# A squareplus gate formed on VectorE from PSUM instead of by a linear matrix on TensorE

## The chip, the cores and the metric

One core of one Trainium2 chip runs the kernel. Five engines work beside each other, each through its own instruction queue in order: TensorE (PE) multiplies matrices into PSUM, VectorE (DVE) and ScalarE (ACT) read and write both memories (PSUM and SBUF), GpSimd (POOL) works on SBUF, SyncE (SP) issues the DMAs. The metric is the device time of one execution in microseconds, and less is better. The engines wait for each other by semaphores; a profile records when each instruction ran.

## What is computed

A gated linear attention, then a two-layer MLP whose activation is squareplus. All inputs and the output are float32; the kernel multiplies in float16.

```python
# q, k, v, f_logit: (4, 8, 768, 48)
f = 1.0 / (1.0 + np.exp(-f_logit))
for t in range(S):
    state = f[:, :, t, :, None] * state + np.einsum('bhd,bhe->bhde', k[:, :, t], v[:, :, t])
    y[:, :, t] = np.einsum('bhd,bhde->bhe', q[:, :, t], state)
x = y.transpose(0, 2, 1, 3).reshape(3072, 384)
h = x @ w_in                            # 384 x 2048
g = 0.5 * (h + np.sqrt(h * h + 4.0))
out = g @ w_out                         # 2048 x 384
```

So g = 0.5 h + sqrt(0.25 h^2 + 1). The first term is linear in x, and both kernels differ in where it is formed.

## The kernel before

The 3072 tokens are 24 row blocks of 128, six for each of the four batch entries; two row blocks make a pair, and the MLP works by pairs (256 tokens), 12 of them.

**Attention, for each pair.** `add_logs`: ACT forms the log decays (Exp, then Ln), DVE splits them into a high and a low float16 part (`lhi`, L326; `llo`, L329). `add_decays`: PE sums them over the block with a triangular matrix into an h bank (L352 to L359, the "W" work), ACT takes two exponentials of the sums (`ea`, `eap`, L365), POOL multiplies them into q and k (`qk`, L371), DVE casts v (L377) and copies small sums (`nls`, L381). `add_attention`, for each row block: q and k are transposed, by PE and a DVE copy (L464, L468) for blocks below `XBAR_FROM` = 10, by a DMA issued by SP (L453) from there on; PE forms the scores (L488), DVE masks them (`pm`, L494), PE forms y (L509, L511), DVE casts it (L516), and it is transposed in turn (PE L544 and DVE L547, or DMA L535) into `xT`. `add_state` carries the state on (L563, L566, L572).

**MLP, for each pair.** `add_mlp1`, called M1 here: PE makes 48 matmuls of 256 columns (L652) into PSUM tiles `hps` of two banks; ACT squares a tile (L660, 1024 columns) and takes the root of two squared tiles (L668, 2048 columns). That root is the `g` tile: the linear half of the gate is not in it. `add_mlp2`, called M2: for each row block 16 matmuls with w_out (L686), and ahead of them three with `w_lin` (L683), all into one PSUM sum `o`; DVE evicts it (L694), SP stores it (L698).

**The linear matrix.** w_lin = 0.5 w_in w_out (384x384) is made once on the chip: `add_transposed_w_in` transposes w_in by PE (L598) and copies it (L604); `add_linear_part` multiplies (L621) and scales (L627). M2 of the first row block waits for it.

**PSUM** has eight banks: h has two tiles of two banks, "a" (all of the attention) two, o two. **The order** of the work is made ahead of time by the class `Plan`: every operation has an engine, a planned duration, a due time, and rings of buffers that it takes and frees, and `Plan.run` gives each engine's queue the ready operation that can start first, the one with the earlier due time among near ones. ACT has two tables of functions, one for Exp and Ln and one for Sqrt; the attention's ACT work is bundled in stretches by `GROUPS` to change tables seldom (L742, L744). Loads go through rings of four buffers (three for f), issued by SP in a fixed order with the weights between the first pairs; an SP instruction that waits holds up those behind it.

Of the kernel before, what the change touches and what calls it, by code (L numbers as in the profile page):

```python
# [15 lines left out]
GROUPS = [[0], [1], [2], [3], [4, 5], [6, 7], [8, 9], [10, 11]]  # L16

XBAR_FROM = 10

PACE = 15.5  # L20
LEAD = {"W": 45.0, "B": 26.0, "M1": 0.0, "M2": -30.0}


class Op:
    __slots__ = ("eng", "dur", "deps", "emit", "due", "allocs", "uses", "end", "kind", "dma", "ins")

    def __init__(self, eng, dur, emit, deps=(), due=0.0, allocs=(), uses=(), kind=None, dma=None, ins=()):
        self.eng, self.dur, self.emit, self.due, self.kind, self.dma = eng, dur, emit, due, kind, dma
# [18 lines left out]
class Plan:  # L47
# [33 lines left out]
    def run(self):  # L81
# [6 lines left out]
        for k in self.queues:  # L88
            by_eng.setdefault(k[0], []).append(k)
        stretch = None  # L90
        loose = False
        while left:
            best = None
            for eng, ks in by_eng.items():
                now = free.get(eng, 0.0)
                cands = []
                for k in ks:
                    if heads[k] < len(self.queues[k]):
                        op = self.queues[k][heads[k]]
                        t = self.ready(op)  # L100
# [11 lines left out]
                if eng == "ACT" and stretch is None and not loose:  # L112
# [38 lines left out]
            t, op, k, eng = best  # L151
            dur = op.dur
# [24 lines left out]
def kernel(  # L177
# [51 lines left out]
    w_lin = konst.tile([128, NJ, DM], FP16, name="w_lin")  # L229
# [14 lines left out]
    P = Plan()  # L244
    T = {}
# [27 lines left out]
    def add_weight(which, i):  # L273
# [17 lines left out]
        def cast():  # L291
            st = T["w", which, i]
            if which == "in":
                nc.vector.tensor_copy(out=w_in16[:, :, i * 256:(i + 1) * 256], in_=st.rearrange("p (j n) -> p j n", j=NJ))  # L294
            else:
                nc.vector.tensor_copy(out=w_out16[:, 2 * i:2 * i + 2, :], in_=st.rearrange("p (j n) -> p j n", j=2))

        w_ready[which, i] = P.add("wcast", "DVE", 0.55, cast, deps=[l], due=-10.0, uses=[buf])

# [8 lines left out]
    def add_logs(p, g):  # L308
# [16 lines left out]
        def d1():  # L325
            nc.vector.tensor_copy(out=lhi[p % NL][:, :, :, 0:D], in_=T["ls", p])  # L326

        def d2():
            nc.vector.tensor_tensor(out=llo[p % NL][:, :, :, 0:D], in0=T["ls", p],  # L329
# [4 lines left out]
        o1 = P.add("logs", "DVE", 0.6, d1, deps=[a2], due=due, allocs=[hl_b], uses=[ls_b])  # L334
        lg[p] = P.add("logs", "DVE", 1.0, d2, deps=[o1], due=due, uses=[ls_b])

    def add_decays(p, g):

        due = vtime(p, "W")
        h_b = Buf(ring("h", 2))  # L340
# [6 lines left out]
        def m1():  # L347
            h = pp_h.tile([128, 2, 512], FP32, name="hps", tag="hps")
            T["ca", p] = h
            for r in range(PR):  # L350
                ca = h[:, r, 0:H * D]
                nc.tensor.matmul(out=ca, lhsT=wcent, rhs=lhi[p % NL][:, r, :, 0:D], start=True, stop=False)  # L352
                nc.tensor.matmul(out=ca, lhsT=wcent, rhs=llo[p % NL][:, r, :, 0:D], start=False, stop=True)
            for r in range(PR):
                nl = h[:, r, H * D:H * D + 2 * NP].rearrange("p (j s) -> p j s", s=2)
# [421 lines left out]
```

## Time and profile before

| | us |
|---|---|
| median of 3 runs | 242.16 (242.06 to 242.81) |
| the profiled execution | 242.64 |
| its span | 240.9 |
| PE busy | 209.4 |
| ACT busy | 149.2 |
| DVE busy | 134.4 |
| POOL busy | 47.6 |

The span runs from the first to the last instruction of the profiled execution. A busy time is the time in which at least one instruction of that engine ran. Matmuls overlap in the pipeline, so their single durations add up to more than the engine's busy time, and the pace is better read from the chain of work, where a row says how long a run of matmuls kept the chain. The idle time before a group of instructions is put down to whatever came last.

### The profile page before, as it was taken

Reading aid. Unit: us, or ns where it says so; the run is one execution under the profiler, and the core shown is the slowest. Engines: PE = TensorE matmul, PEld = TensorE weight load, DVE = VectorE, ACT = ScalarE, POOL = GpSimd, SP = SyncE. Lnnn points to the kernel's source line nnn. Section 1 sums busy time; section 2 is a strip of 40 time slices with the busy share of each in tenths; the row PEclk is TensorE's granted clock in tenths of the full one; section 3 lists DMA queues with packets and bytes.
Section 4 is the critical chain, followed back from the end, with each engine's and each line's share of the span. In section 5 each row is a group of like instructions: output and inputs, shape, how many; then the busy total and the mean of one; then the engine's idle time right before and its main releaser. Section 6 shows DMA issues by size and latency. Waiting matters only on the chain.

```text
span 240.9 us, 4922 instructions
## 1 busy us (share of the span) xinstructions
PE 209.4 (87%) x2038; PEld 151.1 (63%) x2038; DVE 134.4 (56%) x243; ACT 149.2 (62%) x143; POOL 47.6 (20%) x36
## 2 busy tenths in 40 slices
PE   0372698799999994999599999999999999999994
PEld 0151575667668563677487577786678777777662
DVE  5559987866659759665941788435551444100110
ACT  4331264920499939946999399985399665667500
POOL 4236000130014164054100560005230000000000
PEclk9997587799999999799999999999999999999998
DMA  7999998999999979999996433331843111110011
GB/s 147 220 230 304 303 377 187 205 203 183 195 199 217 212 183 221 189 198 214 202 172 124 95 77 84 88 64 49 137 94 62 34 52 49 49 35 33 33 68 65
DMA packets 129302, 35.25 MB, mean 146 GB/s; under 512 B 121088, under 2 KB 129280, under 8 KB 129280
## 3 DMA queue, kind: packets, MB, share of 16 engines
q1 hardware_dynamic: 129280, 34.94, 65.9%
q8 instruction: 16, 0.26, 0.4%
q14 instruction: 6, 0.05, 0.1%
HBM read 25.17 MB, written 4.72 MB: 124 GB/s over the span
## 4 chain that ended last, share of the span: by engine, by line
PE 74%; DVE 12%; ACT 3%; issue 3%; DMA 3%; POOL 2%; SPq 1%; POOLq 0%; ACTq 0%
PE o L686 25%; PE hps L652 24%; PE o L683 5%; PE sc L488 4%; PE wl L621 3%; DVE pm L494 2%; PE tr L464 2%; DVE lhi L326 2%; PE y L511 2%; POOL qk L371 2%; DMA ld_q<-in_q_dram 2%; DVE v L377 1%; PE hps L352 1%; DVE w_in L294 1%; PE wtp L598 1%
## 5 line engine op out<-in xcount | busy, mean ns | idle before, releaser
L652 PE MATMUL hps<-xT,w_in 128*128 128x256 f16 x576 | 75.5, 279 | 5.2 <-ACT hsq L660 4.2
L686 PE MATMUL o<-w_out,g 128*128 128x384 f16 x384 | 73.9, 326 | 0.0
L660 ACT ACTIVATE hsq<-hps 128x1024 f16<-128x1024 f32 x48 | 48.3, 1018 | 36.1 <-PE hps L652 35.6
L652 PEld LDWEIGHTS <-w_in 128*128 128x128 f16 x576 | 55.9, 100 | 17.2 <-issue 5.1
L686 PEld LDWEIGHTS <-g 128*128 128x128 f16 x384 | 35.8, 98 | 20.5
L371 POOL TENSOR_TENSOR qk<-ld_q,ea 128x768 f16<-128x768 f32 x12 | 21.9, 1827 | 128.4 <-ACT ea L365 106.0
L668 ACT ACTIVATE g<-hsq 128x2048 f16<-128x2048 f16 x24 | 45.8, 1910 | 0.6
L494 DVE TENSOR_TENSOR pm<-sc,mask 128x512 f16<-128x512 f32 x48 | 31.9, 686 | 18.4 <-PE sc L488 18.3
L694 DVE COPY o_sb<-o 128x384 f32<-128x384 f32 x24 | 13.3, 556 | 40.3 <-PE o L686 39.8
L365 ACT ACTIVATE ea<-hps 128x768 f32<-128x768 f32 x12 | 9.7, 811 | 27.2 <-PE hps L359 27.2
L371 POOL TENSOR_TENSOR qk<-ld_k,eap 128x768 f16<-128x768 f32 x12 | 23.2, 1936 | 0.0
L516 DVE CAST y<-y 128x384 f16<-128x384 f32 x24 | 13.3, 554 | 17.3 <-PE y L511 17.2
L488 PE MATMUL sc<-qkT 48*128 48x128 f16 x192 | 15.5, 227 | 2.7 <-DVE xT L547 1.4
L683 PE MATMUL o<-w_lin,xT 128*128 128x384 f16 x72 | 15.9, 330 | 0.0
L488 PEld LDWEIGHTS <-qkT 48*128 48x128 f16 x192 | 8.8, 97 | 10.8 <-issue 10.0
L318 ACT ACTIVATE ld_f<-ld_f 128x768 f32<-128x768 f32 x12 | 10.1, 838 | 8.8 <-DMA ld_f<-in_f_logit_dram 8.8
L352 PE MATMUL hps<-lhi,wcent 128*128 128x384 f16 x24 | 8.6, 358 | 6.9 <-DVE lhi L326 6.9
L572 DVE TENSOR_TENSOR sn<-u,gam 128x384 f16<-128x384 f32 x20 | 11.0, 552 | 6.2 <-PE u L566 6.2
L511 PE MATMUL y<-v,pm 128*128 128x48 f16 x192 | 11.7, 185 | 1.1 <-DVE pm L494 1.1
L464 PE MATMUL tr<-ident,qk 128*128 128x128 f16 x80 | 7.7, 257 | 5.6 <-POOL qk L371 4.1
L326 DVE CAST lhi<-ls 128x768 f16<-128x768 f32 x12 | 11.0, 913 | 2.9 <-ACT ls L323 2.9
L511 PEld LDWEIGHTS <-pm 128*128 128x128 f16 x192 | 10.0, 98 | 3.1 <-issue 2.0
(58 smaller groups left out, 221.6 us busy)
## 6 DMA issues: line engine op xcount, KB each, us to landing
ld_f<-in_f_logit_dram SPq DMA_DIRECT2D x24, 192.0 KB, 3.8
ld_q<-in_q_dram SPq DMA_DIRECT2D x24, 192.0 KB, 3.8
ld_k<-in_k_dram SPq DMA_DIRECT2D x24, 192.0 KB, 4.0
ld_v<-in_v_dram SPq DMA_DIRECT2D x24, 192.0 KB, 3.9
out_dram<-o_sb SPq DMA_DIRECT2D x24, 192.0 KB, 1.9
ld_q<-in_moe_w_in_dram SPq DMA_DIRECT2D x3, 384.0 KB, 5.9
ld_k<-in_moe_w_in_dram SPq DMA_DIRECT2D x3, 384.0 KB, 6.1
ld_q<-in_moe_w_out_dram SPq DMA_DIRECT2D x3, 384.0 KB, 8.1
```

Of the source, the lines that this page charges most:

```text
L326: nc.vector.tensor_copy(out=lhi[p % NL][:, :, :, 0:D], in_=T["ls", p])
L371: nc.gpsimd.tensor_tensor(out=qk[p % NB][:, :, i, :, 0:D], in0=T[name, p], in1=T[e, p], op=ALU.mult)
L488: nc.tensor.matmul(out=t[:, j, :], lhsT=qkT[o:o + D, NP + j, :], rhs=qkT[o:o + D, j, :], start=True, stop=True)
L494: nc.vector.tensor_tensor(out=T["pm", r][:, s], in0=T["sc", r, s], in1=mask16.unsqueeze(1).broadcast_to([128, NP, C]), op=ALU.mult)
L511: nc.tensor.matmul(out=y[:, j, s], lhsT=T["pm", r][:, s, j, :], rhs=T["v16", p][:, i, 2 * j + s, :], start=(c == 0), stop=(c == 0 or s == 1))
L516: nc.vector.tensor_copy(out=y16.rearrange("p a b -> p (a b)"), in_=T["y", r].rearrange("p a b d -> p (a b d)"))
L652: nc.tensor.matmul(out=hb[:, a, :], lhsT=w_in16[:, j, jn * 128:(jn + 1) * 128], rhs=T["xT", p][:, j, :], start=(j == 0), stop=(j == NJ - 1))
L660: nc.scalar.activation(out=T["hsq", p, j8][:, j4 % 2], in_=T["h", p, j4].rearrange("p a n -> p (a n)"), func=AF.Square, scale=1.0)
L668: nc.scalar.activation(out=T["g", p][:, 8 * j8:8 * j8 + 8, :].rearrange("p a t -> p (a t)"), in_=T["hsq", p, j8].rearrange("p a n -> p (a ...
L683: nc.tensor.matmul(out=T["o", p, i], lhsT=T["xT", p][:, j, i * C:(i + 1) * C], rhs=w_lin[:, j, :], start=(j == 0), stop=False)
L686: nc.tensor.matmul(out=T["o", p, i], lhsT=T["g", p][:, jn, i * C:(i + 1) * C], rhs=w_out16[:, jn, :], start=False, stop=(jn == NN - 1))
L694: nc.vector.tensor_copy(out=T["o_sb", p, i], in_=T["o", p, i])
```

## The change

The matrix w_lin goes, with the transposes of w_in, the product, its three matmuls in each row block of M2 and two evictions. M1's PSUM tiles become single banks in a ring of five (`NH`), freed later: ACT squares each bank (512 columns), takes the root of a pair of banks (1024 columns) into a tile `r16`, and DVE then forms the gate in one instruction from the bank and the root (L666 of the changed kernel). The o ring shrinks from two banks to one (`NO`). The decays' sums take two of the five h banks, and their exponentials are cut in two. XBAR_FROM goes from 10 to 14, so four more row blocks are transposed by PE. Some operations may run on one of two or three engines, `"DVE|ACT|POOL"` with a planned duration for each, and the planner gives them to the one that would finish first. Tiles are taken by the instruction that begins a step (PE's) instead of the one that writes them. Groups and lead times of the decays change. The core of the diff:

```diff
-GROUPS = [[0], [1], [2], [3], [4, 5], [6, 7], [8, 9], [10, 11]]
-XBAR_FROM = 10
+GROUPS = [[0], [1], [2], [3], [4], [5, 6], [7, 8], [9, 10], [11]]
+XBAR_FROM = 14
-LEAD = {"W": 45.0, "B": 26.0, "M1": 0.0, "M2": -30.0}
+LEAD = {"W": 30.0, "B": 26.0, "M1": 0.0, "M2": -30.0}
+GATE = 10.0
+NH, NA, NO = 5, 2, 1
...
+                own = [c for c in cands if c[2][0].split("|")[0] == eng]
+                kept = []
+                for c in cands:
+                    if c[2][0].split("|")[0] != eng:
+                        first = c[2][0].split("|")[0]
+                        c[1].eng = first
+                        t1 = max(free.get(first, 0.0), self.ready(c[1])) + c[1].durs[first]
+                        c[1].eng = eng
+                        if t1 <= c[0] + c[1].durs[eng] + 0.1 or any(o[0] <= c[0] + 0.2 for o in own):
+                            continue
+                    kept.append(c)
...
-    pp_h = ctx.enter_context(tc.tile_pool(name="pp_h", bufs=2, space=PSUM))
-    pp_a = ctx.enter_context(tc.tile_pool(name="pp_a", bufs=2, space=PSUM))
-    pp_o = ctx.enter_context(tc.tile_pool(name="pp_o", bufs=2, space=PSUM))
+    pp_h = ctx.enter_context(tc.tile_pool(name="pp_h", bufs=NH, space=PSUM))
+    pp_a = ctx.enter_context(tc.tile_pool(name="pp_a", bufs=NA, space=PSUM))
+    pp_o = ctx.enter_context(tc.tile_pool(name="pp_o", bufs=NO, space=PSUM))
...
-        w_ready[which, i] = P.add("wcast", "DVE", 0.55, cast, deps=[l], due=-10.0, uses=[buf])
+        w_ready[which, i] = P.add("wcast", "DVE|ACT|POOL", {"DVE": 0.5, "ACT": 0.75, "POOL": 0.9}, cast, deps=[l], due=-1.0, uses=[buf])
...
-        o1 = P.add("logs", "DVE", 0.6, d1, deps=[a2], due=due, allocs=[hl_b], uses=[ls_b])
-        lg[p] = P.add("logs", "DVE", 1.0, d2, deps=[o1], due=due, uses=[ls_b])
+        o1 = P.add("hi", "DVE|POOL", {"DVE": 0.6, "POOL": 0.9}, d1, deps=[a2], due=due, allocs=[hl_b], uses=[ls_b])
+        lg[p] = P.add("lo", "POOL|DVE", {"DVE": 1.0, "POOL": 1.9}, d2, deps=[o1], due=due, uses=[ls_b])
...
-                nc.scalar.activation(out=t.rearrange("p r h d -> p r (h d)"), in_=T["ca", p][:, :, 0:H * D],
-                                     func=AF.Exp, scale=sign)
+                for r in range(PR):
+                    nc.scalar.activation(out=t[:, r].rearrange("p h d -> p (h d)"), in_=T["ca", p, r][:, 0:H * D],
+                                         func=AF.Exp, scale=sign)
...
-        d1 = P.add("v16", "DVE", 0.6, vc, deps=[ld["v", p]], due=due, allocs=[v_b], uses=[ld_buf["v", p]])
+        v_op = P.add("v16", "POOL|DVE", {"DVE": 0.6, "POOL": 0.9}, vc, deps=[ld["v", p]], due=due, allocs=[v_b], uses=[ld_buf["v", p]])
...
-        yc_op = P.add("Y", "DVE", 0.55, yc, deps=[o], due=due + 4.0, allocs=[y16_b], uses=[a_b])
+        yc_op = yc_ops[r] = P.add("Yc", "DVE|ACT", {"DVE": 0.55, "ACT": 0.5}, yc, deps=[o], due=due + 4.0, uses=[a_b])
...
-    wiT = {}
-    def add_transposed_w_in():
...
-    def add_linear_part(t_ops):
...
+        for j4 in range(4):
+            hsq_b, r_b = Buf(ring("hsq", 2)), Buf(ring("r16", 2))
+            sq, h_bs = [], []
+            for a in range(2):
+                j2 = 2 * j4 + a
+                h_b = Buf(ring("h", NH))
+                h_bs.append(h_b)
...
+                    nc.scalar.activation(out=T["hsq", p, j4][:, a], in_=T["h", p, j2], func=AF.Square, scale=1.0)
...
+                nc.scalar.activation(out=T["r16", p, j4], in_=T["hsq", p, j4], func=AF.Sqrt, scale=0.25, bias=1.0)
...
+                    nc.vector.scalar_tensor_tensor(out=T["g", p][:, jn:jn + 2, :].rearrange("p a t -> p (a t)"),
+                                                   in0=T["h", p, 2 * j4 + a], scalar=0.5, in1=T["r16", p, j4][:, a],
+                                                   op0=ALU.mult, op1=ALU.add)
+                go = P.add("G", "DVE", 0.65, gate, deps=[ro], due=due + 3.6 * j4 - GATE,
+                           allocs=[g_b] if a == 0 and j4 == 0 else [], uses=[r_b, h_bs[a]])
...
-                        for j in range(NJ):
-                            nc.tensor.matmul(out=T["o", p, i], lhsT=T["xT", p][:, j, i * C:(i + 1) * C],
-                                             rhs=w_lin[:, j, :], start=(j == 0), stop=False)
...
-            oo = P.add("o", "DVE", 0.55, oc, deps=[last], due=due - 20.0, allocs=[os_b], uses=[o_b])
+            oo = oc_op[p, i] = P.add("ev", "DVE|ACT", {"DVE": 0.55, "ACT": 0.5}, oc, deps=[last], due=due - 20.0, allocs=[os_b], uses=[o_b])
```

In the planner's new lines, an operation's first-named engine is its own; another takes it only where it would end earlier there and has no work of its own ready.

Where the change moves instructions, first DVE's queue in the first 50 us. Before, at the end of the weight casts (`w_out`), with the copies of the transposed w_in (`wiT`) and the scaling of `w_lin` behind them:

```order
L494 TENSOR_TENSOR pm<-sc,mask_80 128x512
L296 CAST w_out_95<-ld_v 128x768
L494 TENSOR_TENSOR pm<-sc,mask_80 128x512
L296 CAST w_out_95<-ld_q 128x768
L604 COPY wiT<-wtp 128x768
L296 CAST w_out_95<-ld_k 128x768
L516 CAST y_612<-y 128x384
L604 COPY wiT<-wtp 128x768 x7
```

Now, at the same stage of the work (`g` is the gate, `r` the root):

```order
L612 TENSOR_TENSOR sn<-u,gam_108 128x384
L666 SCALAR_TENSOR_TENSOR g_476<-hps,r_451 128x512 x2
L553 CAST y_479<-y 128x384
L612 TENSOR_TENSOR sn<-u,gam_108 128x384
L666 SCALAR_TENSOR_TENSOR g_476<-hps,r_505 128x512 x2
L588 COPY xT<-yt 128x3x128
L553 CAST y_540<-y 128x384
L666 SCALAR_TENSOR_TENSOR g_476<-hps,r_554 128x512 x2
L588 COPY xT<-yt 128x3x128
L326 CAST w_out_95<-ld_k 128x768
```

The copies of wiT have gone, and pair 0's gates stand between the attention steps of the next row blocks, the first of them ahead of DVE's four casts of w_out.

Second, ACT's queue where a stretch of exponentials ends and the MLP goes on (`hsq` is the square). Before:

```order
L660 ACTIVATE hsq<-hps 128x1024
L744 ACT_TABLE_LOAD
L668 ACTIVATE g_1650<-hsq 128x2048
L660 ACTIVATE hsq<-hps 128x1024 x2
L668 ACTIVATE g_1650<-hsq 128x2048
```

Now:

```order
L649 ACTIVATE hsq<-hps 128x512 x2
L741 ACT_TABLE_LOAD
L658 ACTIVATE r_2365<-hsq 128x1024
L649 ACTIVATE hsq<-hps 128x512 x2
L658 ACTIVATE r_2426<-hsq 128x1024
```

Squares and roots are half as wide and twice as many, and a root writes `r16`, which DVE reads, instead of the tile that M2 reads. The queue has 16 table loads now, 14 before.

Third, SP's queue around the last loads. Before:

```order
L266 DMA ld_f<-in_f_logit_dram 128x8x48 x2
L453 DMA_TRANSPOSE qkT<-qk_98 128x8x128 x2
L266 DMA ld_q<-in_q_dram 128x8x48 x2
L698 DMA out_dram<-o_sb 128x384
L266 DMA ld_k<-in_k_dram 128x8x48 x2
L266 DMA ld_v<-in_v_dram 128x8x48 x2
```

Now:

```order
L698 DMA out_dram<-o_sb 128x384 x2
L296 DMA ld_q<-in_q_dram 128x8x48 x2
L296 DMA ld_k<-in_k_dram 128x8x48 x2
L296 DMA ld_v<-in_v_dram 128x8x48 x2
L484 DMA_TRANSPOSE qkT<-qk_99 128x8x128 x2
L698 DMA out_dram<-o_sb 128x384
```

The first DMA transposes stood between the loads; now they stand behind the last one.

On POOL 18 instructions come on: seven casts of v, five of weights and six lo subtractions. ACT takes six evictions of o, three casts of y and two of w_in. In PE's queue the next row block's M2 begins right behind the last one's, with no other PE work between, at seven of the 23 changes of block, the last three among them.

## Rows read from the trace of the kernel before

**Rows 1.** The page's busy us, share of the span and instructions, by engine.
```profile
PE 209.4 (87%) x2038; PEld 151.1 (63%) x2038; DVE 134.4 (56%) x243; ACT 149.2 (62%) x143; POOL 47.6 (20%) x36
```

**Rows 2.** Windows by stage: start:end, length, busy us (instructions), granted clock, DMA, GB/s.
```profile
0.00:45.00 45.00, 24.20 (x245) 17.91 (x246) 34.99 (x66) 18.85 (x21) 10.58 (x16) 0.85 0.98 249
45.00:225.00 180.00, 172.94 (x1719) 125.98 (x1719) 97.19 (x174) 127.48 (x122) 37.01 (x20) 0.98 0.63 128
225.00:240.90 15.90, 12.28 (x76) 7.17 (x74) 2.23 (x4) 2.90 (x2) 0.00 (x0) 0.96 0.18 63
```

**Rows 3.** Windows of 20 us, the same columns.
```profile
60.00:80.00 20.00, 20.00 (x206) 14.37 (x204) 14.35 (x24) 16.13 (x16) 3.59 (x2) 1.00 0.98 201
80.00:100.00 20.00, 15.69 (x151) 11.00 (x151) 14.31 (x24) 15.46 (x18) 7.97 (x4) 0.91 1.01 208
100.00:120.00 20.00, 17.84 (x205) 13.05 (x204) 13.60 (x25) 14.09 (x16) 7.18 (x4) 1.00 0.98 197
...
140.00:160.00 20.00, 19.89 (x202) 14.84 (x201) 12.89 (x26) 18.02 (x19) 3.37 (x2) 1.00 0.41 88
```

**Rows 4.** The chain that ended last: start us, us, what (x matmuls).
```profile
29.42 3.76 PE hps L652 x24
...
47.43 1.31 PE wtp L598 x12
...
50.88 6.50 PE wl L621 x40
...
61.89 0.65 PE o L686 x4
...
76.00 0.89 PE tr L464 x16
...
108.62 2.77 DMA ld_k<-in_k_dram
...
224.27 0.66 PE hps L652 x6
224.93 0.49 PE o L683 x3
...
237.31 0.56 DVE o_sb L694
```

**Rows 5.** Instruction groups by shape: out<-in, count, busy us, mean ns, idle before.
```profile
L660 ACT ACTIVATE hsq<-hps 128x1024 f16<-128x1024 f32 x48 | 48.3, 1018 | 36.1 <-PE hps L652 35.6
L668 ACT ACTIVATE g<-hsq 128x2048 f16<-128x2048 f16 x24 | 45.8, 1910 | 0.6
...
L494 DVE TENSOR_TENSOR pm<-sc,mask 128x512 f16<-128x512 f32 x48 | 31.9, 686 | 18.4 <-PE sc L488 18.3
...
L516 DVE CAST y<-y 128x384 f16<-128x384 f32 x24 | 13.3, 554 | 17.3 <-PE y L511 17.2
...
L326 DVE CAST lhi<-ls 128x768 f16<-128x768 f32 x12 | 11.0, 913 | 2.9 <-ACT ls L323 2.9
...
L365 ACT ACTIVATE ea<-hps 128x768 f32<-128x768 f32 x12 | 9.7, 811 | 27.2 <-PE hps L359 27.2
```

**Rows 6.** Timelines of ACT, DVE, POOL, SP: start us, us, instruction, idle before.
```profile
65.69 1.28 ACT L744 ACT_TABLE_LOAD   x1
66.99 1.91 ACT L668 ACTIVATE g<-hsq 128x2048 f16<-128x2048 f16 x1
...
73.36 1.75 DVE L326 CAST lhi<-ls 128x768 f16<-128x768 f32 x1 [0.42 <-ACT ls L323]
...
76.02 0.55 DVE L326 CAST lhi<-ls 128x768 f16<-128x768 f32 x1
...
72.87 1.82 POOL L371 TENSOR_TENSOR qk<-ld_k,eap 128x768 f16<-128x768 f32 x1
...
103.22 3.19 SPq L453 DMA_TRANSPOSE qkT<-qk  x2
```

**Rows 7.** Waits on PE by DVE: us in total, times, longest.
```profile
DVE pm L494 <- PE sc L488: 18.3, 21, 2.4
```

More of the change, by code (lines that the diff above doesn't have):

```diff
@@ L88, in run @@
         for k in self.queues:
-            by_eng.setdefault(k[0], []).append(k)
+            for e in k[0].split("|"):
+                by_eng.setdefault(e, []).append(k)
         stretch = None
@@ L244 @@
     P = Plan()
+    eng_of = {"DVE": nc.vector, "POOL": nc.gpsimd}
+    cp = {"DVE": nc.vector.tensor_copy, "POOL": nc.gpsimd.tensor_copy, "ACT": nc.scalar.copy}
     T = {}
@@ L456, in add_attention @@
         else:
-            a_b = Buf(ring("a", 2))
+            a_b = Buf(ring("a", NA))
             def tp():
+                new("qkT", [128, 2 * NP, C], FP16, 3)
                 tr = pp_a.tile([128, 2 * NP, C], FP16, name="tr", tag="a")
@@ L610 @@
-    lin_ops = []
-    def add_linear_part(t_ops):
-        for j in range(NJ):
-            o_b = Buf(ring("o", 2))
-            last = None
-            for n in range(4):
-                def mm(j=j, n=n):
-                    if n == 0:
-                        T["wl", j] = pp_o.tile([128, DM], FP32, name="wl", tag="o")
-                    for jn in range(4 * n, 4 * n + 4):
-                        nc.tensor.matmul(out=T["wl", j], lhsT=wiT[jn // 8][:, jn % 8, j * 128:(j + 1) * 128],
-                                         rhs=w_out16[:, jn, :], start=(jn == 0), stop=(jn == NN - 1))
-                last = P.add("M2", "PE", 0.66, mm, deps=t_ops[4 * (n // 2):4 * (n // 2) + 4] + [w_ready["out", 2 * n], w_ready["out", 2 * n + 1], last],
-                             due=5.0, allocs=[o_b] if n == 0 else [], uses=[bufs["wiT", n // 2]])
-            def sc(j=j):
-                nc.vector.tensor_scalar(out=w_lin[:, j, :], in0=T["wl", j], scalar1=0.5, scalar2=None, op0=ALU.mult)
-            lin_ops.append(P.add("o", "DVE", 0.55, sc, deps=[last], due=5.0, uses=[o_b]))
+        o = P.add("KV", "PE", 0.34, kv, deps=[dec[p][0], dec[p][1], state_op.get(r), gm[r]], due=due, allocs=[a_b, sn_b], uses=uses)
@@ L631 @@
+        state_op[r + 1] = P.add("KV", "DVE", 0.55, dk, deps=[o], due=due, uses=[a_b])
     g_ops = {}
+    oc_op = {}
+    yc_ops = {}
     def add_mlp1(p):
@@ new lines, in add_mlp1, with half, square, root @@
+        for j4 in range(4):
[5 more added lines that the diff above has]
+                h_bs.append(h_b)
+                def half(j2=j2):
+                    T["h", p, j2] = pp_h.tile([128, 512], FP32, name="hps", tag="hps")
+                    hb = T["h", p, j2].rearrange("p (a t) -> p a t", a=2)
+                    for a in range(2):
+                        jn = 2 * j2 + a
+                        for j in range(NJ):
+                            nc.tensor.matmul(out=hb[:, a, :], lhsT=w_in16[:, j, jn * 128:(jn + 1) * 128],
+                                             rhs=T["xT", p][:, j, :], start=(j == 0), stop=(j == NJ - 1))
+                def square(a=a, j2=j2, j4=j4):
+                    if a == 0:
+                        T["hsq", p, j4] = sp.tile([128, 2, 512], FP16, name="hsq", tag="hsq", bufs=2)
+                    nc.scalar.activation(out=T["hsq", p, j4][:, a], in_=T["h", p, j2], func=AF.Square, scale=1.0)
+                o = P.add("M1", "PE", 0.66, half, deps=xT_ops[p] + [w_ready["in", j2]], due=due + 1.8 * j2,
+                          allocs=[h_b], uses=[bufs["xT", p]])
+                sq.append(P.add("M", "ACT", 0.54, square, deps=[o], due=due + 1.8 * j2,
+                                allocs=[hsq_b] if a == 0 else [], uses=[h_b]))
+            def root(j4=j4):
+                T["r16", p, j4] = sp.tile([128, 2, 512], FP16, name="r16", tag="r16", bufs=2)
+                nc.scalar.activation(out=T["r16", p, j4], in_=T["hsq", p, j4], func=AF.Sqrt, scale=0.25, bias=1.0)
+            ro = P.add("R", "ACT", 1.06, root, deps=sq, due=due + 3.6 * j4 + 1.8, allocs=[r_b], uses=[hsq_b], kind=("M", 0))
+            for a in range(2):
+                def gate(a=a, j4=j4):
+                    if a == 0 and j4 == 0:
+                        T["g", p] = sp.tile([128, NN, TB], FP16, name="g16", tag="g", bufs=4)
+                    jn = 4 * j4 + 2 * a
+                    nc.vector.scalar_tensor_tensor(out=T["g", p][:, jn:jn + 2, :].rearrange("p a t -> p (a t)"),
[3 more added lines that the diff above has]
+                           allocs=[g_b] if a == 0 and j4 == 0 else [], uses=[r_b, h_bs[a]])
+            g_ops[p].append(go)
```

194 lines of the change are left out of this document (77 added, 117 removed).

## The prediction

> **What bounds the kernel now.** I began with the busy shares of the page [rows 1]: TensorE (PE) is busy for 209.4 us of 240.9, ScalarE (ACT) 149.2, VectorE (DVE) 134.4, GpSimd (POOL) 47.6. A share is an average, so the windows by stage came next [rows 2]. Until 45 us, while data arrive, PE is busy for only 24.2 us and DVE for 35.0 of 45. From 45 to 225 PE works for 172.9 of 180 us, ACT for 127.5 and DVE for 97.2: there PE is the bound, and what leaves PE's queue there shortens the span, if the others keep up. From 225 on only M2 (the second matmul) and its stores are left. The chain that ended last agrees, since from 45 us on it is mostly PE pieces [rows 4]. The one other soft place is 80 to 120 us, where PE idles for 4.3 and 2.2 us [rows 3] and the chain runs through a load of k [rows 4].
>
> The profiled execution took 242.64 us, its span 240.9; 1.74 us lie around it. The median of the three runs is 242.16, so I add 1.74 to a span and take off 0.48 for the time to be forecast.
>
> **What leaves PE.** Three things. The linear term in M2 (L683): 24 row blocks with three matmuls each, 0.49 us for three [rows 4], 11.8 us; 20 of the blocks (9.8 us) lie ahead of the last M1 (the first matmul), 4 (2.0 us) behind. The product w_in by w_out (L621): 48 matmuls at 6.50 / 40 us, 7.8 us. The transposes of w_in (L598): 48, at 1.31 us for 12, 5.2 us [rows 4]. PE works without a break there and the chain runs through all three, so I count them in full: 24.8 us. What is late next at 50 us is M2 of pair 0, whose gates and weights are there by then, and M1 of pair 1, which stand in the order in their place; so the hole gets filled.
>
> **What PE gains.** Row blocks 10 to 13 are now transposed on PE instead of by DMA. 16 transposes of q and k took 0.89 us [rows 4], so a block's 8 cost 0.45, its 3 of y about 0.25: 2.8 us for four. A single o bank: the first M2 quarter of a row block must wait until the last block's sum is evicted. One eviction takes 0.56 us [rows 4], with the handover some 0.65. In the new order 7 of the 23 changes of block have no other PE work between them, three of these in the tail: 4.6 us if nothing hides them, 2.6 of it ahead of the last M1. PE alone then gives 240.9 - 24.8 + 2.8 + 4.6 = **223.5 us**. Bounds for the bank: 0, were all of it covered (the tail's three can't be), to twice that if evictions stand behind other work in the DVE queue.
>
> **What moves ahead of the first M1.** M1 begins at 29.4 us [rows 4], behind a string of DVE work. Two y casts of 0.55 us [rows 5] go from there to ACT, which idles: -1.1 us. Weight casts leave as well, but the loads that feed them are no faster (the DMA engines are 98% busy until 45 us [rows 2]), so I count nothing for them; bounds 0 and -2.2 (twice the y casts).
>
> **The load stream.** At 103.2 us the SP queue issued two DMA transposes, which took 3.19 us, between loads [rows 6], and at 108.6 the chain stands on a load of k [rows 4]. Now all loads are issued ahead of the first DMA transpose. That can give back up to the 6.5 us that PE idled from 80 to 120 [rows 3], or nothing, if the loads then wait for buffers that a busier ACT frees later. I take half: -3.2.
>
> **What ACT and DVE gain.** The gate: 96 DVE instructions that read 128x512 float32 from PSUM and a float16 operand from SBUF. The mask product pm has the same shape and types, 686 ns [rows 5]: 65.9 us. Up to 8 evictions for the transposes on PE add at most 5.5 at the same price. Some 40 DVE instructions go (wiT, w_lin, and casts, lo subtractions and evictions handed to ACT and POOL), at 0.55 us or more each [rows 5], 22 us. DVE rises from 134 to about 183 us. On ACT each long instruction is cut in two. Between 768 columns (811 ns) and 1024 (1018) a column costs 0.81 ns [rows 5], so about 0.19 us of each is fixed: 48 more squares 9.1 us, 24 more roots 6.0 (1910 ns for 2048 leaves 0.25), 24 more exponentials 4.6. Eleven casts and evictions add some 6, and two more table loads 2.6 (1.28 each, and the next instruction starts 1.30 us after the load began [rows 6]). ACT rises from 149 to about 177 us.
>
> The Trainium skill (ScalarE: Activation LUTs, What ACT_TABLE_LOAD costs) puts a switch of tables at about 2.66 us, a drain included; this trace doesn't show the drain, and by the page the two loads would cost ACT 5.3 us instead of 2.6.
>
> How much of this reaches the end? By PE, the last M1 would end at 224.9 - 22.8 (9.8 + 7.8 + 5.2) + 2.8 + 2.6 - 1.1 - 3.2 = 203.2 us. ACT would have about 150 us of work from 43.9 us (45 - 1.1) on: 127.5 [rows 2] plus 23, since the rest of the 28 falls ahead. Its densest window of the four is 18.02 of 20 us, 90% [rows 3]; at that share it needs 167 us, until 210.9, 7.7 later than PE. Five h banks and M2 work in hand let PE run ahead of ACT, so I take half, **+3.8**; bounds 0 and 7.7. The tail stays as it was: 16.0 us from the last M1 to the end [rows 4], less 2.0 for the linear term, plus 2.0 for the o bank.
>
> Sum: 223.5 - 1.1 - 3.2 + 3.8 = **223.0 us** of span, 224.7 as a run, **224.3** against the median.
>
> **Rivals.** *B, the covers hold better.* The load stream stops stalling PE, the mid-run o waits lie under other work, and ACT is never late: 223.5 - 1.1 - 6.5 - 2.6 = 213.3 of span, 214.6. For it: PE did 172.9 of 180 us in the long stage [rows 2], so its order was followed closely. Against it: all three engines would stand near 85% of the span, which only PE does now [rows 1].
>
> *A, ACT (or DVE beside it) is the bound.* If ACT can only be kept busy at the mean of its windows 60 to 80 and 140 to 160, (16.13 + 18.02) / 40 = 85% [rows 3], it needs 150 / 0.85 = 176 us, the last M1 ends at 220 and the span is 236, 237.4. For it: the exponent stretches, in which ACT stands between M1 and the roots, number eight as against seven, and in each ACT waits for PE and DVE. Against it: much of ACT's idle time before was PE's slowness, and that shrinks.
>
> *D, POOL blocks DVE.* The cast lhi took 0.55 us at 76.0, but 1.75 at 73.4, where POOL had an instruction running from 72.9 to 74.7 [rows 6]. The change puts 18 more instructions on POOL. If each held a DVE instruction up by the full 1.2 us, DVE would have 21.6 us more: about 163 us from 43.9 on, at 90% 181, the last M1 at 225 and the span at 241, 242.3: no change. Against it: the mean of lhi is 913 ns [rows 5], so a third of the full delay was usual; and pm, like the gate, kept its 686.
> The Trainium skill says the same of the mechanism (SBUF — State Buffer, Who interferes with whom): VectorE's two-port copies and GpSimd exclude each other for a whole instruction, while a VectorE instruction with one SBUF input does not meet GpSimd at all. By that rule the casts handed to POOL save DVE little, and the gate is safe; the rows agree on both.
>
> *C, the ring of h banks turns into the bound, and the kernel is slower.* A bank is now freed by the gate, not by the square. Least hold: two fills of 0.66 [rows 4], square 0.6, root 1.06, gate 0.69, about 3.7 us; the decays' 24 holds need some 3.3 (79 bank-us). Five banks from 29.4 us to the old last M1 at 224.9 give 978 bank-us, so the ring decides against the change once the mean hold of M1's 96 banks passes (978 - 79) / 96 = 9.4 us. The exponent stretches add about 2.3 (8 of them, each two table loads and some eight instructions of 0.8 us, 9 us on three banks, over 96), so it takes 3.4 us more on every gate, from standing in the DVE queue behind attention steps that wait for PE. At 4 us the last M1 ends at 29.4 + (79 + 96 x 10) / 5 = 237 and the span is 253, 254. Against it: pm, the commonest of such waiters, waited 21 times, 18.3 us in all, 2.4 at the longest [rows 7].
>
> That the change doesn't do what it says can be left out: the orders show the gates, and no linear matrix.
>
> **How the numbers follow.** The forecast case (219 to 229) gets 0.52; B (below 219) 0.17; A (229 to 241.4) 0.17; D (about no change) 0.04; C (slower) 0.10. The likeliest is 224.3. The range 214 to 239 leaves out 0.04 of B, 0.02 of A, and D and C, 0.20 together. Within 0.3% (0.7 us) a measurement of this kernel can't be told from no change: faster 0.52 + 0.17 + 0.17 = 0.86, same 0.04, slower 0.10.
>
> **What would show it.** PE: no wtp and wl rows, M2 of pair 0 near 46 to 50 us instead of 61.9 [rows 4]; the last M1 at 203 to 207; PE busy for some 183 us. The gate at 0.65 to 0.70 us; squares near 0.60, roots near 1.07. In the tail three gaps on PE of about 0.65 us between row blocks. If A holds, PE's longest waits name squares or gates and ACT's share from 45 us on passes 85% with PE under 85%; if D, lhi, v and gi grow well past their means; if C, M1 waits for the gate with DVE waiting for PE. B shows as PE above 96% from 45 us to the last M1. I am wrong from the start if PE finds no work in the hole at 50 us: then PE's gap there stays and the gain is some 13 us smaller.

## The result, and the profile after

| | before | after |
|---|---|---|
| median, us | 242.11 (241.91 to 242.81) | 230.98 (228.29 to 231.78) |
| the profiled execution, us | 242.64 | 230.96 |
| its span, us | 240.9 | 229.2 |

The ratio of the times is 0.950, with an interval of 0.942 to 0.958. The change gains 11 us at the medians. I had forecast 224.3, a gain of 17.8, with a range of 214 to 239: the direction and the range hold, the size is 6.7 us off. The time lies where rival A was (229 to 241).

The page of the changed kernel begins with the busy us, share and instructions of each engine, and then shows the span in 40 slices (tenths busy, and tenths of the full TensorE clock):

```profile
PE 196.0 (86%) x1914; PEld 141.7 (62%) x1914; DVE 174.0 (76%) x321; ACT 167.4 (73%) x253; POOL 67.1 (29%) x54
...
PE   0355989887878979989899599999999999999873
...
PEclk9998579997967997999999999999999999999999
```

Against [rows 1], DVE has 39.6 us more and ACT 18.2. PE has only 13.4 us less, although by my prices 24.8 us of its work are gone and 2.8 came. The windows say where. Their columns are start:end, length, busy us (instructions) of PE, its weight loads, DVE, ACT, POOL, then granted clock, DMA share, GB/s. First the changed kernel:

```profile
0.00:45.00 45.00, 28.89 (x283) 21.19 (x284) 33.77 (x69) 26.40 (x40) 16.23 (x22) 0.89 0.93 241
45.00:80.00 35.00, 29.70 (x284) 20.84 (x282) 26.70 (x51) 25.99 (x42) 12.72 (x8) 0.85 0.99 200
80.00:150.00 70.00, 63.77 (x692) 47.33 (x690) 61.35 (x110) 59.29 (x93) 33.57 (x22) 0.98 0.76 160
150.00:205.00 55.00, 55.00 (x541) 40.48 (x539) 44.77 (x81) 46.47 (x68) 4.59 (x3) 1.00 0.29 65
```

and the kernel before, in the two stretches in the middle:

```profile
45.00:80.00 35.00, 34.81 (x340) 25.35 (x340) 24.77 (x46) 20.50 (x22) 7.19 (x4) 0.95 1.00 201
80.00:150.00 70.00, 63.13 (x670) 45.55 (x669) 45.87 (x82) 54.31 (x57) 22.65 (x12) 0.98 0.83 164
```

From 150 us on PE works without a break in both, until the tail. The difference is between 45 and 80: where the old PE idled for 0.2 us of 35, the new one idles for 5.3, and the granted clock falls from 0.95 to 0.85 beside it. The idle time is in many small pieces. From the timeline of PE there (start, duration, what, matmuls, idle before and what ended it; rows between are left out):

```profile
47.31 0.81 PE L683 MATMUL o<-w_out,g 128*128 128x384 f16 x4 [0.65 <-DVE o_sb L694]
47.96 2.78 PE L643 MATMUL hps<-xT,w_in 128*128 128x256 f16 x24
...
52.38 0.84 PE L522 MATMUL sc<-qkT 48*128 48x128 f16 x8 [0.86 <-DVE qkT L500]
53.91 0.82 PE L643 MATMUL hps<-xT,w_in 128*128 128x256 f16 x6 [0.69 <-DVE g L666]
...
63.95 0.34 PE L585 MATMUL yt<-ident,y 128*128 128x128 f16 x3 [1.00 <-ACT y L551]
...
67.28 2.74 PE L643 MATMUL hps<-xT,w_in 128*128 128x256 f16 x12
```

No gap is longer than 1 us, and they have several releasers. At 67.28 twelve matmuls of M1 took 2.74 us, where at 47.96 twenty-four took 2.78. That is the lower of TensorE's two clock levels (1.2 instead of 2.4 GHz), called the half clock below; it is inside "busy", not inside "idle". The windows around it:

```profile
60.00:66.00 6.00, 3.92 (x40) 2.39 (x40) 5.96 (x14) 2.52 (x5) 3.27 (x2) 0.93 1.13 223
66.00:73.00 7.00, 6.63 (x67) 5.04 (x66) 2.83 (x6) 3.51 (x5) 0.71 (x1) 0.57 0.75 172
```

What PE waited for in all, from the waits of PE between 43 and 152 us (total, times, longest), the largest first (its longest wait, 1.3 us, lies behind 120 us) and one that matters for rival C:

```profile
PE o L683 <- DVE o_sb L694: 3.6, 5, 1.3
...
PE hps L643 <- DVE g L666: 0.7, 1, 0.7
```

The groups that answer to [rows 5] (columns as there):

```profile
L649 ACT ACTIVATE hsq<-hps 128x512 f16<-128x512 f32 x96 | 54.4, 587 | 24.0 <-PE hps L643 23.9
L666 DVE SCALAR_TENSOR_TENSOR g<-hps,r 128x512 f16<-128x512 f32 x96 | 61.8, 683 | 9.4 <-ACT r L658 9.2
...
L658 ACT ACTIVATE r<-hsq 128x1024 f16<-128x1024 f16 x48 | 50.7, 1057 | 1.4
...
L526 DVE TENSOR_TENSOR pm<-sc,mask 128x512 f16<-128x512 f32 x48 | 32.1, 684 | 5.8 <-PE sc L522 5.5
...
L356 DVE CAST lhi<-ls 128x768 f16<-128x768 f32 x12 | 14.1, 1175 | 2.9 <-ACT ls L353 2.8
```

And the end of the chain of waits, which answers to the last rows of [rows 4]:

```profile
211.96 0.66 PE hps L643 x6
212.62 2.77 PE o L683 x16
215.42 0.49 ACT o_sb L692
215.95 2.77 PE o L683 x16
218.75 0.57 DVE o_sb L694
219.36 2.77 PE o L683 x16
222.21 0.57 DVE o_sb L694
222.82 2.77 PE o L683 x16
```

The last M1 ends at 212.62 us (forecast 207.0) and the tail takes 16.6 (forecast 16.0). So most of the miss arose ahead of the tail, and the stretch that differs most from before is 45 to 80 us. Over the whole span PE idles for 33.2 us now and 31.5 before (the spans less PE's busy times), since it idles less until 45 us. What fell short of my terms as a whole is the drop of PE's busy time, 13.4 us instead of 22.0 (24.8 less 2.8).

### The profile page after: what moved, and what is told of

Same layout as the page of the kernel before. It is cut to its first block, busy times and chain, and to the rows that moved or that the text cites. A ratio compares the mean times of both kernels' runs of the same rounds, so it can differ in the third digit from the quotient of the medians.

```text
span 229.2 us, 4909 instructions
## 1 busy us (share of the span) xinstructions
PE 196.0 (86%) x1914; PEld 141.7 (62%) x1914; DVE 174.0 (76%) x321; ACT 167.4 (73%) x253; POOL 67.1 (29%) x54
## 4 chain that ended last, share of the span: by engine, by line
PE 59%; DVE 15%; DMA 9%; issue 5%; SPq 5%; ACT 2%; POOL 2%; POOLq 0%; DVEq 0%; ACTq 0%
PE o L683 24%; PE hps L643 19%; SPq L296 5%; PE sc L522 4%; DMA ld_q<-in_moe_w_out_dram 3%; DVE pm L526 3%; DVE lhi L356 3%; DMA out_dram<-o_sb 2%; PE tr L496 2%; DVE o_sb L694 2%; DVE qkT L500 2%; DMA ld_q<-in_q_dram 2%; POOL qk L401 2%; DMA ld_f<-in_f_logit_dram 2%; DVE gi L442 2%
## 5 line engine op out<-in xcount | busy, mean ns | idle before, releaser
L649 ACT ACTIVATE hsq<-hps 128x512 f16<-128x512 f32 x96 | 54.4, 587 | 24.0 <-PE hps L643 23.9
L666 DVE SCALAR_TENSOR_TENSOR g<-hps,r 128x512 f16<-128x512 f32 x96 | 61.8, 683 | 9.4 <-ACT r L658 9.2
L658 ACT ACTIVATE r<-hsq 128x1024 f16<-128x1024 f16 x48 | 50.7, 1057 | 1.4
L694 DVE COPY o_sb<-o 128x384 f32<-128x384 f32 x18 | 10.0, 556 | 18.4 <-PE o L683 17.5
L522 PE MATMUL sc<-qkT 48*128 48x128 f16 x192 | 17.5, 230 | 5.2 <-DVE pm L526 1.6
L356 DVE CAST lhi<-ls 128x768 f16<-128x768 f32 x12 | 14.1, 1175 | 2.9 <-ACT ls L353 2.8
L395 ACT ACTIVATE ea<-hps 128x384 f32<-128x384 f32 x24 | 10.5, 488 | 7.8 <-PE hps L388 7.5
L407 POOL CAST v<-ld_v 128x768 f16<-128x768 f32 x7 | 6.4, 913 | 29.3 <-DMA ld_v<-in_v_dram 10.0
L496 PE MATMUL tr<-ident,qk 128*128 128x128 f16 x112 | 10.5, 254 | 4.1 <-POOL qk L401 4.1
L359 POOL TENSOR_TENSOR llo<-ls,lhi 128x768 f16<-128x768 f32 x6 | 9.9, 1644 | 9.3 <-DVE gam L451 7.7
```

Of the source, the lines that this page charges most:

```text
L356: cp[o1.eng](out=lhi[p % NL][:, :, :, 0:D], in_=T["ls", p])
L496: nc.tensor.transpose(out=tr[:, s * NP + j, :], in_=qk[p % NB][:, i, s, 2 * j:2 * j + 2, :], identity=ident16)
L522: nc.tensor.matmul(out=t[:, j, :], lhsT=qkT[o:o + D, NP + j, :], rhs=qkT[o:o + D, j, :], start=True, stop=True)
L649: nc.scalar.activation(out=T["hsq", p, j4][:, a], in_=T["h", p, j2], func=AF.Square, scale=1.0)
L658: nc.scalar.activation(out=T["r16", p, j4], in_=T["hsq", p, j4], func=AF.Sqrt, scale=0.25, bias=1.0)
L666: nc.vector.scalar_tensor_tensor(out=T["g", p][:, jn:jn + 2, :].rearrange("p a t -> p (a t)"), in0=T["h", p, 2 * j4 + a], scalar=0.5, in1= ...
```

## The experiments

Each ratio is against the kernel before, run beside it on the same chip. The changed kernel has 0.950 (0.942 to 0.958); 0.01 is 2.4 us. It was not run again beside its variants, so differences between them of less than 2 us lie within the intervals.

**What was the removed PE work worth?** Three kernels leave parts of the linear term out of the kernel before, whose order of instructions stays. e1 leaves out all three parts:

```diff
 def tp():   # transposes of w_in, their copies, the product, its scaling
-    ... nc.tensor.transpose / matmul ...
+    pass
 def quarter():
-    3 x nc.tensor.matmul(o, xT, w_lin)
```

> The kernel before, in its own order, with the linear term left out: no transposes of w_in, no product w_in by w_out, no linear matmuls in the second matmul (the output lacks the term 0.5 h). ACT keeps its long squares and roots, the banks their pairs. It prices the 24.8 us of PE work by itself. Theory S (the forecast's first term): the order closes up and the time falls by 22 to 26 us, to 216 to 220 us. Rival: part of it becomes new idle time of PE, since squares, roots and loads do not come sooner; then 222 us or more, with PE waits on hsq above the 3.5 us of before.

0.940 (0.932 to 0.947): 14.5 us of the 24.8, at most 16.4 by the interval. Theory S, the first term of my sum, is refuted. The time is the rival's, but its sign is missing: PE's waits for squares are 4.2 us on the page of e1 as on that of the kernel before. Which part is not worth its time? f1 leaves out the transposes and the product alone (w_lin is set to zero), f2 the linear matmuls alone.

> The kernel before, in its own order, without the transposes of w_in and the product w_in by w_out, 13.0 us of PE work around 50 us; the linear matmuls stay and read a matrix of zeros (the term 0.5 h is left out of the output). Theory L (until some 80 us PE can only do what the load stream has brought; that work filled a hole): the hole stays, 238 to 242 us. Theory S (the order closes up, as the forecast counted): 228 to 231 us.

0.981 (0.976 to 0.985): 4.7 us of 13.0, at most 5.8; 237.3 us lies between the two theories, far nearer to L.

> The kernel before, in its own order, without the 72 linear matmuls of the second matmul (11.8 us; 0.5 h is left out of the output); the transposes and the product stay, unused. Theory L and theory S agree if most of the 72 lie behind 120 us, where PE works without a break: 230 to 233 us. Rival (what is freed there waits for squares or evictions instead): 236 us or more. With f1 it says where the 24.8 us went: the two gains should add up to the 13.3 of e1.

0.956 (0.951 to 0.960): 10.7 us of 11.8. The two add up to 15.4, beside 14.5 for both at once. So the linear matmuls gave what was counted for them, and the product with its transposes only a third. The trace of f1 shows what took the place of the 13 us. Its page, and PE's timeline where they stood:

```profile
PE 201.3 (85%) x1942; PEld 144.5 (61%) x1942; DVE 131.5 (56%) x232; ACT 149.2 (63%) x143; POOL 48.5 (21%) x37
...
46.89 1.47 PE L641 MATMUL hps<-xT,w_in 128*128 128x256 f16 x6
49.09 0.61 PE L465 MATMUL tr<-ident,qk 128*128 128x128 f16 x4 [0.74 <-POOL qk L372]
50.86 0.61 PE L465 MATMUL tr<-ident,qk 128*128 128x128 f16 x4 [1.16 <-POOL qk L372]
51.27 0.52 PE L353 MATMUL hps<-lhi,wcent 128*128 128x384 f16 x1
52.27 0.48 PE L354 MATMUL hps<-llo,wcent 128*128 128x384 f16 x1 [0.48 <-DVE llo L330]
...
55.88 0.43 PE L489 MATMUL sc<-qkT 48*128 48x128 f16 x4
```

The same two steps, M1 and the scores, in the kernel before:

```profile
57.55 0.82 PE L652 MATMUL hps<-xT,w_in 128*128 128x256 f16 x6
...
60.90 0.39 PE L488 MATMUL sc<-qkT 48*128 48x128 f16 x4
```

ACT's timeline ahead of it:

```profile
43.12 1.91 ACT L657 ACTIVATE g<-hsq 128x2048 f16<-128x2048 f16 x1
45.04 1.28 ACT L731 ACT_TABLE_LOAD   x1
46.34 0.81 ACT L366 ACTIVATE ea<-hps 128x768 f32<-128x768 f32 x1
```

POOL's:

```profile
47.23 1.81 POOL L372 TENSOR_TENSOR qk<-ld_q,ea 128x768 f16<-128x768 f32 x1 [25.16 <-ACT ea L366]
49.00 1.80 POOL L372 TENSOR_TENSOR qk<-ld_k,eap 128x768 f16<-128x768 f32 x1
```

and the windows of f1 there:

```profile
45.00:57.00 12.00, 8.71 (x66) 5.61 (x66) 8.54 (x14) 5.51 (x8) 3.58 (x2) 0.57 1.07 212
57.00:80.00 23.00, 22.50 (x230) 15.69 (x229) 16.18 (x29) 19.10 (x20) 5.18 (x3) 1.00 1.02 209
```

The M1 group that ran behind the product in the kernel before (at 57.55 us) now runs at 46.89, 10.7 earlier. The next step, the transposes of q and k, has a chain of its own: root, table load, exponentials on ACT, then two products on POOL of 1.8 us each. PE takes that chain's results as they come, with gaps of 0.74, 1.16 and 0.48 us, and does the little that it has until 57 us at a granted clock of 0.57. The scores behind it (sc) start at 55.9 us, which is 5.0 earlier than before instead of 13. In the kernel before, the product was the work that covered this chain. Over the whole span PE's busy time fell by 8.1 us for the 13.0 and its idle time grew by 2.8, so more of the loss shows as busy time than as waiting.

**Was it ACT, DVE, or both?** e2 makes the gate light (a copy of the root, SBUF to SBUF), e3 halves the columns of squares and roots, g4 does both. The order of instructions is that of the changed kernel in all three.

```diff
 # e2
-nc.vector.scalar_tensor_tensor(out=g, in0=h, scalar=0.5, in1=r16, op0=ALU.mult, op1=ALU.add)
+nc.vector.tensor_copy(out=g, in_=r16)
 # e3: hsq and r16 have 256 columns for 512
-nc.scalar.activation(out=hsq[:, a], in_=h, func=AF.Square, scale=1.0)
+nc.scalar.activation(out=hsq[:, a], in_=h[:, 0:256], func=AF.Square, scale=1.0)
```

> The changed kernel, same order, but each gate only copies the root from SBUF to SBUF in float16 instead of adding 0.5 h from PSUM (the output lacks 0.5 h). DVE loses an estimated 40 us of its 174, and the h bank is freed by the square. Theory Q (PE's 11.5 us of idle time between 45 and 150 come from attention steps and sums that stand behind gates in the DVE queue): the idle time falls by half or more and the time to 221 to 226 us. Rival A (ACT is the bound): no change within 1%, 229 to 232. Rival H (PE's stalls are the bare hand-overs, whatever DVE's load): 228 to 231.

0.946 (0.940 to 0.953), some 1 us better than the changed kernel and not to be told from it, although DVE's busy time fell by 31 us to 142.9. Theory Q, which asked for 221 to 226, fails; 228.7 is where rival H had it. (In e2 and e3, Q is DVE's queue; in the runs below it is bare hand-overs between engines.)

> The changed kernel, same order, but squares and roots work on half of their columns (256 of 512, 512 of 1024), and each gate reads its 256 roots twice, so ACT loses an estimated 40 us of its 167 (the other half of the activation is left out). Theory Q: ACT is not the bound, so at most 3 us are gained, 227 to 231. Rival A (ACT sets the pace of the long stage): the last first matmul moves to where PE alone would put it, some 9 us earlier, 219 to 223.

0.944 (0.940 to 0.947), 1.5 us better, with ACT at 128.2 us instead of 167.4. Rival A, which asked for 9 us here, is refuted.

> The changed kernel, same order, with the light gate of e2 and the light squares and roots of e3 together (half of the activation and 0.5 h are left out), so that DVE and ACT have about the work that they had before the change. If DVE and ACT share the blame (each alone hides the other): 5 us or more off, 222 to 225.5 us. Theory O: little more than either alone, 226.5 to 229 us.

0.936 (0.932 to 0.941), 3.3 us better than the changed kernel; the intervals just don't meet. Each alone is within the changed kernel's interval, and both together give a little more than the sum of the two (2.4). Its page and its stretch from 45 to 80 us:

```profile
PE 192.8 (86%) x1914; PEld 139.3 (62%) x1914; DVE 138.7 (62%) x321; ACT 128.6 (57%) x253; POOL 66.7 (30%) x54
...
45.00:80.00 35.00, 28.33 (x285) 19.22 (x284) 26.82 (x52) 23.25 (x43) 13.62 (x9) 0.90 1.01 202
```

With DVE near and ACT below the load that each had before the change, PE still idles for 6.7 us there. The load of the two is worth some 3 us of the whole, as theory O had it (226.5 to 229), and in this order it is not what makes the hole.

**Was it the load stream?** f3 loads q, k and v of one row block for two, from pair 2 on:

```diff
-for r in range(PR):
+for r in range(1 if p >= 2 and name != "f" else PR):
     nc.sync.dma_start(out=t[:, r], ...)
```

> The changed kernel, same order, but from pair 2 on q, k and v are loaded for the first row block of a pair only, and the second one uses the same rows (the second row block's data are left out): three eighths of the stream of those pairs are gone, all engine instructions stay. Theory L: pairs 2 to 5 come earlier, PE's waits between 45 and 100 us shrink to less than half, and the time falls to 219 to 226 us. Rival Q (stalls are hand-overs inside an order that doesn't fit, whatever the loads do): 229 to 232 us.

0.956 (0.952 to 0.960): no gain, as rival Q had it. The stretch from 45 to 80 us in f3:

```profile
45.00:80.00 35.00, 29.83 (x287) 21.03 (x285) 28.05 (x52) 25.33 (x41) 13.87 (x9) 0.85 0.69 146
```

The DMA engines' share falls from 0.99 to 0.69, and PE's busy time from 45 to 80 us is that of the changed kernel within 0.2 us. In this order earlier q, k and v gain nothing, although the DMA engines were busy for 0.99 of that stretch. g3 lets the planner count on the shorter loads:

> As f3 (second row block's q, k, v from pair 2 on not loaded), but the planner counts these loads at half their time, so that its order makes use of them. Theory O with the loads behind it: 224 to 228 us, where f3 with the old order gave 231.6. If loads don't matter in any order: 230 to 232.

0.945 (0.940 to 0.949), 1.3 us better than the changed kernel by the ratios, whose intervals overlap: whether the loads limit some better order stays open. g1 brings pairs 2 and 3 ahead of w_out instead:

```diff
-ORDER = "P0 P1 i03 f2 i47 o07 qkv2"
+ORDER = "P0 P1 i03 f2 i47 qkv2 f3 o07 qkv3"
```

> The changed kernel with one line of its table changed: q, k, v of pair 2 and all of pair 3 are loaded ahead of w_out instead of behind it (planned anew). Theory O (the hole that the removed product leaves is there because the order has no other PE work ready between 45 and 80 us, as attention of pairs 2 and 3 waits for its data): PE idles there for under 3 us instead of 5.3, and the time falls to 225 to 228.5. Rival Q (bare hand-overs between engines, which every order has): 230 to 232 us.

0.956 (0.952 to 0.960): no gain, PE idles for 6.0 us from 45 to 80 and now waits once, for 1.5 us, for a cast of w_out. Theory O's forecast for this run (under 3 us of idle time) fails: data that come earlier are not enough.

**The single o bank.** e7 has four SBUF buffers for the evicted sums (`bufs=2` becomes 4), in the same order:

> The changed kernel, same order, with four SBUF buffers for the evicted sums instead of two, so that an eviction never waits for a store to land (one did, 0.63 us at 72 us, and PE idled behind it). If that wait and the half clock around it are worth something: 228.5 to 230. If the next hand-over takes its place: no change within 0.3%, 230.5 to 231.5.

0.950 (0.944 to 0.957): the wait for a store was worth nothing that can be measured. f4 gives o its second bank back, at the price of one of h (`NH, NA, NO = 4, 2, 2`), and is planned anew:

> The changed kernel with two banks for the sums and four for h (planned anew). If the single o bank costs what PE's waits for evictions show (6.1 us, 1.6 of it in the tail): 225 to 228 us. If four h banks make the first matmul wait for gates instead: 231 us or more.

0.980 (0.973 to 0.986), 7 us slower. PE's waits for evictions are gone, those for gates are 2.4 us (1.4 of M1, 1.0 of M2), and waits inside the attention grew (one for the state, 3.3 us). It does not price the bank, since its order is another one throughout; it says that another split of the banks with an order of its own can cost 7 us.

**Is it the order?** In g2 only the planner's numbers are different: its durations are those which the profiles show, and the table was chosen anew for them, by the planner's own end time. (The new XBAR_FROM takes the transposes of two row blocks from PE, 1.4 us by the price that the prediction put on four.)

```diff
-XBAR_FROM = 14
-PACE = 15.5
-LEAD = {"W": 30.0, "B": 26.0, "M1": 0.0, "M2": -30.0}
-GATE = 10.0
-ORDER = "P0 P1 i03 f2 i47 o07 qkv2"
+XBAR_FROM = 12
+PACE = 16.5
+LEAD = {'W': 34.0, 'B': 18.0, 'M1': -9.0, 'M2': -30.0}
+GATE = 19.0
+ORDER = 'P0 P1 f2 i07 qkv2 f3 o07 qkv3'
 # planned durations: gate, pm 0.65 -> 0.69; square 0.54 -> 0.60; cast lhi 0.6 -> 1.0; gi 0.2 -> 0.8;
 # ea, eap 0.9 -> 1.0; Exp, Ln 0.8 -> 0.86; a load 2.1 -> 1.85; and smaller ones
```

> The changed kernel with the planner's durations set to those that the profiles show (gate and pm 0.69 us, square 0.60, cast lhi 1.0, load 1.85 and so on) and its table of orders, leads and groups chosen anew for them. Theory O: a better order gets back a good part of the 11.5 us that PE idles between 45 and 150 us: 220 to 226 us. Rival Q: 229 us or more.

0.927 (0.923 to 0.931), 224.54 us at the median, 5.5 us better than the changed kernel, and the fastest of all runs here. Its windows:

```profile
0.00:45.00 45.00, 24.29 (x230) 17.85 (x231) 31.35 (x61) 20.62 (x32) 18.34 (x22) 0.97 1.00 251
45.00:80.00 35.00, 30.74 (x319) 22.89 (x317) 31.34 (x58) 30.47 (x46) 15.04 (x12) 0.99 0.97 199
80.00:150.00 70.00, 68.27 (x725) 49.30 (x725) 60.10 (x112) 62.54 (x96) 31.42 (x23) 1.00 0.78 163
```

From 80 to 150 us PE works for 68.27 us instead of 63.77, and the granted clock hardly falls anywhere. Between 45 and 80 PE idles for 4.3 us, 1.0 less, but does 319 matmuls instead of 284. The engines' work is nearly the same, and more of PE's lies where it was ready: theory O holds for g2, and Q as I had put it (229 us or more in any order) falls. What in g2 does it (the durations, the leads, two blocks fewer to transpose on PE, the load order, which alone did nothing) was not taken apart.

## Why the prediction was right, and where it was wrong

That the range held is in part owed to its width: the time lies outside the forecast case (219 to 229), in the band of rival A, whose mechanism the runs refute.

*What left PE: mis-sized, the step that failed.* I counted 24.8 us in full, "so the hole gets filled". e1 measures 14.5; f2 confirms the linear matmuls (10.7 of 11.8), f1 gives 4.7 for the 13.0 of the product and its transposes. I had named this ("wrong from the start if PE finds no work in the hole at 50 us"), but as all or nothing, gave it no chance of its own, and no case of mine had its price. The evidence that I used was that PE worked there without a break and that the chain ran through the product [rows 4]. Both are true, and neither says what stands behind. The windows did show the risk: until 45 us PE was busy for 24.2 of 45 us [rows 2], that is, the MLP had no stock of work yet, and the product was what PE did while attention was under way. In the changed kernel M2 of pair 0, which I had named to fill the hole near 46 to 50, did come early, at 37.0 us instead of 61.7. It filled idle time ahead of 45 us (PE busy 28.9 us instead of 24.2), and was then missing behind it, where the row shows 5.3 us of idle time and the clock at 0.85. From PE's timeline of the changed kernel, the first M1 and the first M2:

```profile
26.85 2.77 PE L643 MATMUL hps<-xT,w_in 128*128 128x256 f16 x12
...
37.02 0.81 PE L683 MATMUL o<-w_out,g 128*128 128x384 f16 x4
```

That the 8.3 us which f1 lost are lost in the changed kernel too is read from these rows, not measured in its order. One price was also misread. I took the transposes at 1.31 us for 12, at 47.43 [rows 4], where the granted clock was 0.57 (47.0 to 48.7 us). The same chain has them again two microseconds later, where it was 1.00:

```profile
49.39 0.67 PE wtp L598 x12
```

At that price all 48 cost 2.7 us instead of 5.2, and the term is 22.3. In f1, without them, the low clock fell on the work that took their place.

*What PE gained: nearly right.* The o bank cost 6.1 us of waits on the whole page (4.9 for DVE's evictions, 1.2 for ACT's) instead of 4.6, in nine waits for the seven that I counted; in the tail the three gaps were 0.57, 0.65 and 0.70, as counted. Ahead of it 4.2 instead of 2.6.

*Ahead of the first M1.* It began at 26.85 us, 2.6 earlier, where I had counted 1.1. Of the weight casts, for which I had counted nothing, DVE had done two by then instead of four, at 0.94 us each; no run parts them from the y casts.

*The load stream: right in size, the cause not shown.* The 6.5 us of PE idle time between 80 and 120 [rows 3] became 3.1, so 3.4 were gained where I took 3.2. But PE's waits there name squares for 3.5 us before and not at all after, and the squares' banks are part of the change as well. No run put the old order of the loads back.

*ACT and DVE: right in size, not in mechanism.* I gave their coupling +3.8; taking both loads away gains 3.3 (g4). But my sum put it on ACT alone, 7.7 us behind PE, and half of ACT's squares and roots were worth 1.5 us, not to be told from nothing (e3), so that the size fits is partly luck. The prices of the instructions hold: gate 683 ns for a forecast 686, squares 587 for 600, roots 1057 for 1070. Their totals came out lower, DVE 174.0 for 183 and ACT 167.4 for 177.

*The tail: right,* 16.6 for 16.0.

The terms as measured, in place of mine, move 224.3 by +9.4 (24.8 less the 15.4 of f1 and f2), -1.5, +1.5, -0.2 and -0.5: 233.0 for a measured 231.0. Terms that were measured in the old order do not close to better than that in the new one.

*Rivals.* **A** gave the right range for the wrong reason: PE's waits do not name squares, ACT was busy for 137.3 of the 166 us from 45 to 211 (83%), and half its work was worth 1.5 us (e3). **B** fell with the clock and the idle time between 45 and 80: from 45 to 211 PE was busy for 93%, and B asked for 96. **C**: M1 waited 0.7 us for a gate between 43 and 152, so five banks were enough. **D**: the cast lhi grew from a mean of 913 ns to 1175. Beside POOL's timeline (the two engines' rows put together) it shows why:

```profile
107.79 1.65 POOL L359 TENSOR_TENSOR llo<-ls,lhi 128x768 f16<-128x768 f32 x1
107.86 2.00 DVE L356 CAST lhi<-ls 128x768 f16<-128x768 f32 x1
```

Five of the twelve casts began with no POOL instruction running and took 0.54 to 0.56 us; the other seven (0.81 to 2.23 us) began while POOL was at work, and each ended 0.41 to 0.43 us after a POOL instruction. In three of the seven it was work new on POOL (llo twice, v once), and these three lost 3.0 us, about all that lhi grew by. So POOL's new work does hold DVE up. The Trainium skill (SBUF — State Buffer, Who interferes with whom) has it that VectorE's two-port copies and casts and GpSimd shut each other out for a whole instruction, which agrees with the seven. By the same section of the Trainium skill an instruction with one SBUF input, outside the two-port modes, does not meet GpSimd; the gate, with one input from SBUF and one from PSUM, kept its price, between 676 and 692 ns, which agrees as well. But DVE's load hardly reaches the end (e2), so this cost little. The prediction's "the casts handed to POOL save DVE little; the rows agree" was not shown: DVE's total came out 9 us below my sum.

*The sign that I had chosen badly:* "PE busy for some 183 us". My own terms give 187.4 (209.4 - 24.8 + 2.8), and it was 196.0. Part of the excess is the clock: g2, at a mean granted clock of 0.992 instead of 0.947 and with 22 matmuls fewer, has 190.9. The rest was not taken apart. A busy time can't be used as a count of work where the clock changes.

## What to carry to other kernels

Before the time of removed work is counted in full, look at what stands behind it in the queue and when that becomes ready: work that an engine did while it had nothing else is a cover, and taking it away gives back only what the next chain allows (here a third). Where the order is planned from a table of durations, a change that moves load between engines needs the table measured again: here new durations, with a table chosen for them, gave half as much (5.5 us) as the change itself, though what in them did it is open. And read idle time together with the granted clock, for busy time as well as prices: work read at the half clock looks twice as dear.

## What was not expected of the hardware

From 60 to 66 us PE idled for 2.1 us in gaps of at most 1.0, and in the 7 us that followed the granted clock was 0.57; each of TensorE's two levels (1.2 and 2.4 GHz) shows in the matmuls, twelve in 2.74 us at 67.28 against twenty-four in 2.78 at 47.96. Not every such stretch costs time. Two executions of the changed kernel had a span of 229.2 us at mean clocks of 0.947 and 0.976, and e2, whose first 45 us had a clock of 1.00 instead of 0.89, has a span of 229.3. The Trainium skill (TensorE: Matmul & The Clock Gate, Part 1: The HAM clock gate) says that the clock follows how busy PE was of late, which agrees; what a stretch at the low level is worth depends on whether PE is waited for there. A tiny DVE instruction (gi, 4 to 16 columns) took between 148 and 1807 ns, and lhi between 543 and 2230 at one shape, while the 96 gates and 48 pm all took between 674 and 692.
